# Moving two weight loads, one attention output and one LayerNorm by a visit in a fused transformer block

## Chip, cores and metric

One NeuronCore of a Trainium2 chip runs the whole program. The metric is the device time of one execution in microseconds (us). The kernel before took a median of 360.95 us in three runs (360.5 to 361.54).

## What is computed

A pre-norm block: dilated sliding-window attention, then an MLP, each with a residual. S = 2048 tokens, D = 576, 32 heads of 18, F = 4608, all arrays bf16.

```python
def _A_ref(x, wqkv, wo):            # H = 32, W = 8, dilation 2
    q, k, v = (x @ wqkv) ...        # per head
    idx = pos[:, None] - arange(W) * 2      # 8 keys for each token, 2 apart; below 0 masked
    attn = softmax(sum_d(q * k[idx]) * Dh ** -0.5)
    return sum_w(attn * v[idx]) @ wo

def _B_ref(x, w1, b1, w2, b2):
    h = gelu(layernorm(x) @ w1 + b1)
    return h @ w2 + b2

h  = x + _A_ref(layernorm(x), wqkv, wo)
h2 = h + _B_ref(layernorm(h), w1, b1, w2, b2)
```

## The kernel before, in words

**Tiles.** The 2048 tokens are 16 tiles of 128: tile j holds tokens 16p + j on partition p. With a dilation of 2 the eight keys of a token of tile j lie in the tiles of the same parity: at the same partition for tiles up to j, one partition lower for those above. So attention works on a ring of eight tiles (`kv_ring`, one for even and one for odd j), takes the tiles from 14 downwards, and when a tile is done its K and V are replaced by the same rows shifted by one partition, which `halo` (L344) loads from a copy in DRAM (`store_halo`). A halo row is issued by SP when DVE has read the old row, and the next tile's product waits for it.

**Stages.** The first stage makes Q, K and V of all tiles on PE in 24 *visits*, numbered 0 to 23, and meanwhile the attention of the first group (tiles 14 and 12, called A[0] and A[1]) and part of that of A[2]. Then eight groups of two tiles go through the MLP; while PE works on one group, DVE, ACT and the DMAs do the attention and the LayerNorm (LN2) of the next. LN1 of the even tiles is turned on PE (`tr_x`); the odd tiles, normalized on ACT, go to DRAM (`out_x`, L290) and come back transposed, two tiles at a time (`in_x`, L295). Visits 12 to 23 use the odd tiles; the last read, `in_x(3)`, serves visits 21 to 23.

**A visit** (`visit`, L242) works on two or three *pairs*. A pair is one 128x576 product in two PSUM banks; since the contraction is split over two halves of the array's rows, it is done in two halves (`phase`, L221): 10 matmuls, and 8 more in which the banks have changed places. All first halves come first, then a hook (transposes on PE), then the second halves, each followed by the evacuation of its pair on ACT, and by the functions of `between` (behind the first, or the n-th with `{n: ...}`). Because the banks change places, a second half has to stand behind the end of the first. This is done by a *marker* (L237): a no-op on POOL's queue that waits for the last matmul of the first half, and that the first matmul of the second half waits for:

```python
def marker(mm_ins):
    nop = nc.gpsimd.nop().ins
    tc.add_manual_dep(nop, mm_ins.name, sync_dep, reason="end of a half's visit")
```

**Order.** The whole kernel stands in a manual schedule: each engine runs its instructions in the order in which the Python code emits them. For the first stage the order is written in tables by visit: `after` (L944) holds what follows a visit, `loads` (L937) the weight loads issued behind that, `between` (L967), `hooks` (L976), and `wo_with` (L975), which adds the pair of an output projection to a visit. SP issues nearly all DMAs, in order. A weight load also waits for the last evacuation emitted before it (`pace`, L103).

**What the change touches.**
- `load_w1(c)` (L131), c = 0 to 5: 768 KB each. Before, pieces 3 and 4 follow visit 13, piece 5 visit 17.
- Attention output of A[1]: DVE writes o to `q_all` (L414); `o_tail` (L197) copies its last 128 columns on ACT; `tr_o` (L431) turns o on PE into PSUM pair D, and ACT copies it to `oT`. `wo_duo` (L449) multiplies by Wo, also into pair D (`pw`).
- LN2 of A[1]: `ln2` (L478) on DVE adds x to `pw` (`h`, L473) and makes the statistics (L148 to L155) and the negative mean (L487); `ln2_rstd` (L529) makes one power on POOL (L161); `ln2_norm` (L537) scales the mean (L539) and writes `hn` (L174) on ACT; `tr_h` (L554) turns it on PE, ACT copies it to `hnT` (L557), which the MLP of the first group needs.
- QK of A[2] on DVE: the product (`att_qk_a`, L352), four adds (`att_qk_add`, L361), logits, maximum, difference (`att_qk_rest`, L377), then the exponential on ACT (`att_exp`, L393).
- Warm-up matmuls on a constant (`busy`, L833) ahead of the first transposes.

Behind the first stage: `late_wo` and `wo_visit` in the first group's MLP are the output projections of the second group's tiles; their `oT` comes by a store and a transposed read (`dma_tr_o`, L216).

Of the kernel before, what the change touches and what calls it, by code (L numbers as in the profile page):

```python
# [17 lines left out]
def kernel(  # L18
# [12 lines left out]
    nc = tc.nc  # L31
    P = 128
    _, S, D = A_x.shape
# [62 lines left out]
    def psum_pair(tag, name, dtype=F32):  # L96
        n = 512 if dtype == F32 else 1024
        return psum.tile([P, 2, n], dtype, tag=f"ps{tag}", name=name)
# [78 lines left out]
    def transpose_in(pair, src, tail=None):  # L177
        for kt in range(KT):
            c = min(kt * P, D - P)
            block = src[:, c:c + P] if kt < KF or tail is None else tail  # L180
            for r in range(2):
                nc.tensor.matmul(pair[:, r, kt * HP:(kt + 1) * HP], lhsT=block[half_rows(r)],
                                 rhs=ident[half_rows(r), half_rows(r)], start=True, stop=True, skip_group_check=True)
# [17 lines left out]
    def turned(dst, pair, k0=0, k1=KT):  # L201
        return dict(out=dst[:, k0:k1, :].rearrange("p k (r t) -> p r k t", r=2),
                    in_=pair[:, :, k0 * HP:k1 * HP].rearrange("p r (k t) -> p r k t", t=HP))
# [14 lines left out]
    def half_rows(r):  # L218
        return slice(r * HP, (r + 1) * HP)
# [51 lines left out]
    def new_xnT(js):  # L271
        t = qp.tile([P, KT, 2 * P], BF16, tag="xnT", name="xnT", bufs=5)
        for n, j in enumerate(js):
            xnT[j] = t[:, :, n * P:(n + 1) * P]
        return t

    def tr_x(j, tag):
        pair = psum_pair(tag or "CAB"[(ring_pos[0] + 1) % 3], "xt_pt")
        transpose_in(pair, q_all[:, j, :])
        if EVEN.index(j) % 2 == 0:  # L280
            new_xnT(EVEN[EVEN.index(j):][:2])
        for k0, k1 in ((0, 2), (2, KT)) if j in EVEN[0:2] else ((0, KT),):
            nc.scalar.copy(**turned(xnT[j], pair, k0, k1))
# [24 lines left out]
    def qkv_duo(j, t):  # L308
        def make():
            ps = ring_pair("pq")  # L310
            xt = xnT[j]

            def op(g, i, sl, kt):
                c0 = g * HALF
                if g == 0 and kt == KF - 1 and sl.start:
                    kt = KF
                return xt[sl, kt, :], (wq_sb[sl, kt, t * D + c0:t * D + c0 + HALF] if kt < KF else wqh_sb[sl, t, c0:c0 + HALF])

            def evac():
                dst = (q_all[:, j, :], k_ring[j % 2][:, j // 2, :], v_ring[j % 2][:, j // 2, :])[t]  # L320
                scale = dict(scale=rstd_of[j]) if j in EVEN else {}
                pace[0] = nc.scalar.activation(out=dst.rearrange("p (d g h) -> p g d h", g=2, h=H // 2),
                                               in_=ps[:, :, 0:HALF].rearrange("p g (h d) -> p g d h", h=H // 2),
                                               func=ACT.Copy, **scale).ins
                if j == ATT_ORDER[0] and t == 1:
                    store_halo(j, slice(0, 1))
            return dict(g=[[ps[:, r, 0:HALF]] for r in range(2)], op=op, evac=evac)
        return make
# [12 lines left out]
    def logit_of(js):  # L341
        return logits[:, sides(js)]
# [15 lines left out]
    def att_qk_add(j, steps):  # L358
        for o, a, c in steps:
            n = (c - a if c < 9 else 9) * H  # L360
            nc.vector.tensor_tensor(out=prod[:, :, o * H:o * H + n], in0=prod[:, :, a * H:a * H + n],  # L361
                                    in1=prod[:, :, c * H:c * H + n], op=ALU.add)

    def att_qk_b(j, i, skip=0):
        side[j] = i
        out = logit_of([j])[:, 0]
        att_qk_add(j, ((0, 0, 9), (0, 0, 4), (0, 0, 2), (0, 0, 1))[skip:])
        nc.vector.tensor_tensor(out=out, in0=prod[:, :, 0:H], in1=prod[:, :, 8 * H:9 * H], op=ALU.add)
        if j // 2 + 1 < W:
            nc.vector.memset(out[0:1, j // 2 + 1:W, :], -1e9)  # L370
# [332 lines left out]
    def c_(fn, *a):  # L703
        return lambda: fn(*a)
# [96 lines left out]
    def call(fns):  # L801
        for fn in fns:
            fn()

    with tc.manual_schedule(engines={ENG.PE, ENG.Activation, ENG.DVE, ENG.SP, ENG.Pool}):
# [23 lines left out]
        load_w1h()  # L829
        busy = psum_pair("D", "busy")  # L830
        ones = nc.const_aps.tensor(1.0, [P, 512], BF16)
        for n in [512] * 8 + [P] * 5:
            nc.tensor.matmul(busy[:, 0, 0:n], lhsT=ones[:, 0:P], rhs=ones[:, 0:n], start=True, stop=True)  # L833
        nc.gpsimd.memset(mhalf[:], -0.5)
        nc.gpsimd.memset(eps2[:], EPS * EPS)
# [37 lines left out]
        def ln1_even_rstd(*gis):  # L873
            for gi in gis:
                mv, _ = ln1.pop(gi)
                veps = qp.tile([P, 1], F32, tag="ln1_veps", name="ln1_veps", bufs=8)
                nc.vector.tensor_scalar(out=veps[:], in0=mv[:, 0, 1:2], scalar1=1.0, scalar2=EPS, op0=ALU.mult, op1=ALU.add)
                rstd_of[EVEN[gi]] = ln_rstd(veps, f"ln1_{gi}", 1)[:, 0:1]
# [20 lines left out]
        A = ATT_ORDER  # L899
# [35 lines left out]
            ln2_ins(c, d)  # L935

        loads = {}  # L937
        for c, v in enumerate((2, 3, 4, 13, 13, 17)):
            loads[v] = loads.get(v, []) + [c_(load_w1, c)]
        for q, v in enumerate((6, 8, 11, 12)):  # L940
            loads[v] = [c_(load_wo, [q])]
        for n, v in enumerate((19, 19, 20, 20, 21, 22)):
# [11 lines left out]
                c_(store_halo, A[1]), c_(store_halo, A[0], slice(1, 2))],  # L954
            9: [c_(ln1_act, 9, 0)],
            10: [c_(att_pv, A[0]), c_(ln1_act, 9, 1), c_(in_x, 1), c_(halo, A[1], 1)],
            11: [c_(out_x, 2), c_(halo, A[0], 2)],
            12: [c_(ln1_act, 10, 0)],
            13: [c_(ln1_act, 10, 1), c_(in_x, 2), c_(out_x, 3), c_(store_halo, A[2]), c_(store_halo, A[3])],
            14: [c_(att_pv, A[1]), c_(in_x, 3), c_(load, b2_bc, B_b2.partition_broadcast(P))],  # L960
            15: [c_(halo, A[1], 2), c_(o_tail, A[0])],
            17: [c_(o_tail, A[1]), c_(ln2, A[0]), c_(att_qk_a, A[2])],
            18: [c_(ln2_rstd, A[0]), c_(halo, A[2], 1)],
            19: [c_(ln2, A[1])],
            20: [c_(ln2_rstd, A[1]), c_(att_qk_rest, A[2], 0)],
        }
        between = {  # L967
            10: [c_(att_exp, A[0])],
            13: [c_(att_exp, A[1])],
            18: {1: [c_(tr_o, A[1], "D")]},  # L970
            19: {1: [c_(ln2_norm, A[0])]},
            21: [c_(ln2_norm, A[1])],
            22: [c_(att_exp, A[2])],
        }
        wo_with = {17: A[0], 19: A[1]}  # L975
        hooks = {  # L976
            0: {1: lambda: call([c_(tr_x, EVEN[1], "C"), c_(ln1_even, 2)])},
            **{n: {m: c_(tr_x, EVEN[2 * n + m - 1], "D" if m == 1 else None) for m in (1, 2)} for n in (1, 2, 3)},
            12: c_(tr_b1, "D"),
            16: c_(tr_o, A[0], "D"),  # L980
            21: c_(tr_h, A[0], "D"),
            22: c_(tr_h, A[1], "D"),
        }
        seq = [(j, t) for t in (1, 2) for j in EVEN[:2]] + [(j, 1) for j in EVEN[2:]] \
            + [(j, 0) for j in A[0:2]] + [(j, 2) for j in EVEN[2:]] + [(j, 0) for n in (0, 4, 2) for j in EVEN[n:n + 2]] \
# [1 line left out]

        ln1_even_rstd(0, 1)
        tr_x(EVEN[0], "D")
        for qd in range(len(seq) // 2):  # L990
            duos = [qkv_duo(*seq[2 * qd]), qkv_duo(*seq[2 * qd + 1])]
            if qd in wo_with:
                duos.append(wo_duo(wo_with[qd], "D"))
            visit(duos, hooks.get(qd), between.get(qd, ()), apart=qd == 0)
            call(after.get(qd, ()))
            call(loads.get(qd, ()))
# [37 lines left out]
        for k, g in enumerate(GROUPS):  # L1034
            c, d = GROUPS[k + 1] if k + 1 < len(GROUPS) else (None, None)
# [123 lines left out]
```

## Time and profile before

| what | value |
|---|---|
| median of 3 runs | 360.95 us (360.5 to 361.54) |
| profiled execution | 362.23 us, of which the profile's span is 360.4 |
| mean granted PE clock | 0.995 |
| busy: PE, DVE, ACT, POOL | 352.6, 295.9, 235.9, 48.1 us |
| PE busy in 0 to 10 us | 7.55 us |
| PE busy in 52.5 to 68.2 us | 13.68 of 15.70 us |
| start of the first MLP matmul | 68.15 us |

All times in the views count from the start of the span. A timeline row has start, length, engine, source line, operation, output and input, count, and in brackets the time for which the engine was idle ahead of it and what ended that. SPq is the queue of DMAs issued by SP: the length of its rows is that of the issue, not of the transfer. The chain that ended last is followed back from the last instruction; each piece is work on the step that set the end. In the table of stages each row has a window, its length, and the busy time of each engine in it, the granted clock of PE, the share of the 16 DMA engines that was busy, and GB/s.

### The profile page before, as it was taken

Reading aid. Unit: us, or ns where it says so; the run is one execution under the profiler, and the core shown is the slowest. Engines: PE = TensorE matmul, PEld = TensorE weight load, DVE = VectorE, ACT = ScalarE, POOL = GpSimd, SP = SyncE. Lnnn points to the kernel's source line nnn. Section 1 sums busy time; section 2 is a strip of 40 time slices with the busy share of each in tenths; the row PEclk is TensorE's granted clock in tenths of the full one; section 3 lists DMA queues with packets and bytes.
Section 4 is the critical chain, followed back from the end, with each engine's and each line's share of the span. In section 5 each row is a group of like instructions: output and inputs, shape, how many; then the busy total and the mean of one; then the engine's idle time right before and its main releaser. Section 6 shows DMA issues by size and latency. Waiting matters only on the chain.

```text
span 360.4 us, 11550 instructions
## 1 busy us (share of the span) xinstructions
PE 352.6 (98%) x4938; PEld 290.7 (81%) x4938; DVE 295.9 (82%) x416; ACT 235.9 (65%) x524; POOL 48.1 (13%) x61
## 2 busy tenths in 40 slices
PE   7999998999999999999999999999999999999996
PEld 3788886788778877887788778877887788778874
DVE  5999999989889998998799899989998989520431
ACT  4889764898556783668656956695669566706620
POOL 2340005000212020201110202021102110210000
PEclk8999999999999999999999999999999999999999
DMA  7996599972636496732463355344545254283001
GB/s 240 329 294 193 147 258 310 367 253 55 169 66 100 132 244 109 129 79 51 91 102 90 85 124 84 90 86 120 88 90 99 58 85 58 54 120 51 4 1 34
DMA packets 63492, 46.29 MB, mean 128 GB/s; under 512 B 32192, under 2 KB 61760, under 8 KB 63440
## 3 DMA queue, kind: packets, MB, share of 16 engines
q1 hardware_dynamic: 59472, 41.50, 43.6%
q0 software_dynamic: 3744, 3.84, 9.9%
q8 instruction: 38, 0.62, 0.8%
q10 hardware_dynamic: 224, 0.22, 0.3%
q14 instruction: 14, 0.11, 0.1%
HBM read 23.38 MB, written 12.42 MB: 99 GB/s over the span
## 4 chain that ended last, share of the span: by engine, by line
PE 80%; DVE 11%; DMA 5%; ACT 2%; issue 1%; SPq 0%; DVEq 0%; ACTq 0%
PE pm L228 39%; PE po L691 25%; PE po L603 10%; PE pw L228 4%; DMA xnT<-xd 3%; DVE ln_stats L148 2%; DVE prod L361 2%; DVE prod L407 1%; DVE prod L352 1%; PE pq L228 1%; DMA x_all<-in_A_x_dram 1%; DMA wq_sb<-in_A_wqkv_dram 1%; ACT h_all L584 1%; DVE prod L413 1%; DVE ln_mv L149 1%
## 5 line engine op out<-in xcount | busy, mean ns | idle before, releaser
L228 PE MATMUL pm<-hnT,w_sb 64*128 64x256 bf16 x2304 | 143.0, 269 | 0.0
L584 ACT ACTIVATE h_all<-pm,b_sb 128x256 f16<-128x256 f32 (+1 forms) x288 | 108.7, 496 | 51.0 <-PE pm L228 50.3
L228 PEld LDWEIGHTS <-w_sb 64*128 64x128 bf16 x2304 | 111.6, 94 | 15.2 <-issue 1.7
L228 PE MATMUL pq<-wq_sb,xnT 64*128 64x288 bf16 x720 | 55.7, 286 | 3.0 <-DMA xnT<-xd 1.8
L691 PEld LDWEIGHTS <-h_all 128*128 128x128 f16 x480 | 46.2, 98 | 13.7 <-issue 1.6
L228 PEld LDWEIGHTS <-xnT 64*128 64x128 bf16 x864 | 44.7, 95 | 11.9 <-DMA xnT<-xd 2.1
L361 DVE TENSOR_TENSOR prod<-prod 128x2304 bf16<-128x2304 bf16 (+1 forms) x64 | 44.2, 691 | 2.1
L352 DVE TENSOR_TENSOR prod<-kv_ring,q_all 128x4608 bf16<-128x4608 bf16 x16 | 40.8, 2551 | 3.2 <-POOL ln_rstd L498 2.4
L407 DVE TENSOR_TENSOR prod<-kv_ring,probs 128x4608 bf16<-128x4608 bf16 x16 | 40.9, 2558 | 2.2 <-DMA kv_ring<-kv_dram 1.7
L228 PE MATMUL pm<-hnT,w1h_sb 64*128 64x256 bf16 x288 | 39.2, 269 | 0.0
L691 PE MATMUL po<-w2a_sb,h_all 128*128 128x288 bf16 (+1 forms) x262 | 35.9, 286 | 0.0
L413 DVE TENSOR_TENSOR prod<-prod 128x2304 bf16<-128x2304 bf16 (+1 forms) x32 | 33.9, 1058 | 1.1
L603 PEld LDWEIGHTS <-h_all 128*128 128x128 bf16 x288 | 27.9, 98 | 7.9 <-issue 0.9
L691 PEld LDWEIGHTS <-kv_ring 128*128 128x128 f16 x252 | 24.6, 98 | 6.3
L603 PE MATMUL po<-w2a_sb,h_all 128*128 128x288 bf16 x224 | 28.5, 286 | 0.0
L228 PE MATMUL pq<-wqh_sb,xnT 64*128 64x288 bf16 x144 | 28.1, 288 | 0.0
L793 POOL DMA_DIRECT2D x_all<-o_sb x12 | 10.7, 888 | 125.1 <-PE pw L228 72.3
L498 POOL TENSOR_TENSOR ln_rstd<-ln_var,mhalf 128x1 f32<-128x1 f32 x13 | 10.2, 786 | 84.2 <-ACT ln_var L497 84.2
L161 POOL TENSOR_TENSOR ln_rstd<-ln_veps,mhalf 128x1 f32<-128x1 f32 (+2 forms) x14 | 14.1, 1019 | 45.4 <-DVE ln_nmean L487 28.0
L691 PE MATMUL po<-w2b_sb,h_all 128*128 128x288 bf16 (+1 forms) x122 | 19.7, 286 | 0.2 <-DVE h_all L671 0.2
L228 PE MATMUL pw<-wo_sb,oT 64*128 64x288 bf16 x256 | 19.5, 283 | 0.0
L671 DVE TENSOR_TENSOR kv_ring<-h_all 128x1536 f16<-128x1536 f16 (+3 forms) x9 | 6.8, 760 | 15.4 <-ACT h_all L584 15.3
(113 smaller groups left out, 400.3 us busy)
## 6 DMA issues: line engine op xcount, KB each, us to landing
w_sb<-in_B_w_dram SPq DMA_DIRECT2D x6, 768.0 KB, 6.3
kv_ring<-kv_dram SPq DMA_DIRECT2D x28, 144.0 KB, 2.4
kv_dram<-kv_ring SPq DMA_DIRECT2D x13, 288.0 KB, 4.3
x_all<-in_B_b_dram SPq DMA_DIRECT2D x15, 144.0 KB, 3.8
w2a_sb<-in_B_w_dram SPq DMA_DIRECT2D x2, 1008.0 KB, 7.1
td<-q_all SPq DMA_DIRECT2D x14, 144.0 KB, 2.3
td<-hn SPq DMA_DIRECT2D x14, 144.0 KB, 1.8
x_all<-h POOLq DMA_DIRECT2D x14, 144.0 KB, 4.5
```

The source lines that it names most:

```text
L148: nc.vector.bn_stats(out=stats[:, i, c, :], in_=src[:, c * HALF:(c + 1) * HALF])
L161: nc.gpsimd.tensor_tensor(out=rstd[:], in0=veps[:], in1=mhalf[:].to_broadcast([P, n]), op=ALU.pow)
L228: last = nc.tensor.matmul(duo["g"][r ^ swap][i], lhsT=lhsT, rhs=rhs, start=(swap == 0 and i == 0 and kt == 0), stop=(swap == 1 and kt == K ...
L352: ins = nc.vector.tensor_tensor(out=prod[:], in0=k_ring[j % 2], in1=q_all[:, j, :].unsqueeze(1) .to_broadcast([P, W, D]), op=ALU.mult).ins
L361: nc.vector.tensor_tensor(out=prod[:, :, o * H:o * H + n], in0=prod[:, :, a * H:a * H + n], in1=prod[:, :, c * H:c * H + n], op=ALU.add)
L407: nc.vector.tensor_tensor(out=prod[:].rearrange("p w (d h) -> p w d h", h=H), in0=v_ring[j % 2].rearrange("p w (d h) -> p w d h", h=H), in ...
L413: nc.vector.tensor_tensor(out=prod[:, 0:n, :], in0=prod[:, 0:n, :], in1=prod[:, n:2 * n, :], op=ALU.add)
L498: ins = nc.gpsimd.tensor_tensor(out=rstd[:], in0=var[:], in1=mhalf[:], op=ALU.pow).ins
L584: pace[0] = nc.scalar.activation(out=hT(grp)[:, f, 0:N], in_=ps[:, r, i * N:(i + 1) * N], func=ACT.Gelu_apprx_tanh, bias=b1_sb[:, f:f + 1] ...
L603: nc.tensor.matmul(banks[half], lhsT=hT(grp)[:, f, i * P:(i + 1) * P], rhs=w2_rows(f)[:, half * HALF:(half + 1) * HALF], start=(f == 0), s ...
L691: nc.tensor.matmul(bank, lhsT=l, rhs=r, start=start, stop=stop, skip_group_check=True)
L793: nc.gpsimd.dma_start(out=x_of(j), in_=o_of.pop(j), accum_op=ALU.add)
```

## The change

1. W1 piece 3 is issued behind visit 11, right behind `out_x(2)`; piece 4 behind visit 14, after `in_x(3)`. Piece 5 stays at 17.
2. `o_tail` of A[1] moves from the end of visit 17 into visit 18, behind the first pair's evacuation; `tr_o` of A[1] from the end of visit 18 into the hook of visit 19; its wo pair from visit 19 to visit 20.
3. `ln2` of A[1] moves from behind visit 19 to behind visit 20, ahead of its rstd. The first of the four adds of QK of A[2] moves ahead of it (behind visit 18).
4. `tr_h` of A[0] and A[1] move from the hooks of visits 21 and 22 to those of 22 and 23; `ln2_norm` of A[1] from visit 21 to visit 22, behind the exponential of A[2].
5. The warm-up has three more matmuls of 128 columns, and twelve of 64 rows and 128 columns follow the first transposes (`tr_x`).

```diff
+    ADDS = ((0, 0, 9), (0, 0, 4), (0, 0, 2), (0, 0, 1))
 def att_qk_b(j, i, skip=0):
-        att_qk_add(j, ((0, 0, 9), (0, 0, 4), (0, 0, 2), (0, 0, 1))[skip:])
+        att_qk_add(j, ADDS[skip:])
...
-        for n in [512] * 8 + [P] * 5:
+        for n in [512] * 8 + [P] * 8:
             nc.tensor.matmul(busy[:, 0, 0:n], lhsT=ones[:, 0:P], rhs=ones[:, 0:n], start=True, stop=True)
...
-        for c, v in enumerate((2, 3, 4, 13, 13, 17)):
-            loads[v] = loads.get(v, []) + [c_(load_w1, c)]
+        for c, v in ((0, 2), (1, 3), (2, 4), (4, 14), (5, 17)):
+            loads[v] = [c_(load_w1, c)]
...
-            11: [c_(out_x, 2), c_(halo, A[0], 2)],
+            11: [c_(out_x, 2), c_(load_w1, 3), c_(halo, A[0], 2)],
...
-            17: [c_(o_tail, A[1]), c_(ln2, A[0]), c_(att_qk_a, A[2])],
-            18: [c_(ln2_rstd, A[0]), c_(halo, A[2], 1)],
-            19: [c_(ln2, A[1])],
-            20: [c_(ln2_rstd, A[1]), c_(att_qk_rest, A[2], 0)],
+            17: [c_(ln2, A[0]), c_(att_qk_a, A[2])],
+            18: [c_(ln2_rstd, A[0]), c_(halo, A[2], 1), c_(att_qk_add, A[2], ADDS[:1])],
+            20: [c_(ln2, A[1]), c_(ln2_rstd, A[1]), c_(att_qk_rest, A[2], 0, 1)],
         between = {
...
-            18: {1: [c_(tr_o, A[1], "D")]},
+            18: [c_(o_tail, A[1])],
             19: {1: [c_(ln2_norm, A[0])]},
-            21: [c_(ln2_norm, A[1])],
-            22: [c_(att_exp, A[2])],
+            22: [c_(att_exp, A[2]), c_(ln2_norm, A[1])],
-        wo_with = {17: A[0], 19: A[1]}
+        wo_with = {17: A[0], 20: A[1]}
         hooks = {
...
             16: c_(tr_o, A[0], "D"),
-            21: c_(tr_h, A[0], "D"),
-            22: c_(tr_h, A[1], "D"),
+            19: c_(tr_o, A[1], "D"),
+            22: c_(tr_h, A[0], "D"),
+            23: c_(tr_h, A[1], "D"),
...
         tr_x(EVEN[0], "D")
+        busy = psum_pair("B", "busy")
+        for n in range(12):
+            sl = half_rows(n % 2)
+            nc.tensor.matmul(busy[:, n % 2, 0:P], lhsT=ones[sl, 0:P], rhs=ones[sl, 0:P], start=True, stop=True)
```

## Prediction

> **What bounds the kernel now.** I read the page first. PE is busy for 352.6 of 360.4 us, so 7.8 us of idle PE is all that a change of order can win. The stages table puts 2.5 of these in the first 10 us, 2.0 between 52.5 and 68.2, and 3.1 at the end, which the change does not touch. Next I read the chain that ended last, in order of time:
>
> ```profile
> 50.88 0.13 DVE prod L413
> 51.01 9.39 DMA xnT<-xd
> 60.44 1.40 PE pq L228 x20
> ```
>
> Until 50.88 the chain is DVE work almost alone (from 10.52, where x landed). Then one transfer, the last transposed read of the odd x tiles, takes 9.39 us, and PE starts visit 21 on it. From 68.32 to 339.68 the chain is PE without a gap. SP's timeline tells why the transfer is slow (start, length, what):
>
> ```profile
> 48.84 2.00 SPq L104 DMA_DIRECT2D w_sb<-in_B_w_dram  x2
> 51.01 3.86 SPq L296 DMA_TRANSPOSE xnT<-xd  x1
> ```
>
> Two W1 pieces (768 KB each) go out just ahead of it. The other three reads of this kind landed 3.6 to 3.8 us after issue. In PE's timeline (last bracket: idle time ahead of the row and who ended it) I mark the slips between 52 and 68 us:
>
> ```profile
> 52.85 0.29 PE L182 MATMUL o_pt<-ident,q_all 64*128 64x64 bf16 x8
> ...
> 60.44 0.66 PE L228 MATMUL pq<-wq_sb,xnT 64*128 64x288 bf16 x8 [1.75 <-DMA xnT<-xd]
> ...
> 64.56 0.29 PE L188 MATMUL h_pt<-ident,hn 64*128 64x64 bf16 x8
> ...
> 68.15 0.60 PE L228 MATMUL pm<-hnT,w_sb 64*128 64x256 bf16 x8
> ```
>
> A full half of a visit's pair (10 matmuls) takes 0.615, a second half (8) 0.49, tr_o 0.14, tr_h 0.39. Adding these from 52.53, the three starts are late by 0.32 (the copy of o's tail on ACT ends at 52.46), 1.93 (the transfer) and 0.28 (LN2's output from ACT, 64.51): 2.53 us of slip. The first MLP matmul stands at 68.15.
>
> **W1 pieces.** The fourth goes behind out_x(2), at about 39.8, where SP would have stood idle until 42.79; the stages of 40 to 42 and 42 to 44 us show a DMA share of 0.63 and 0.09, room for about 2.5 us of transfer, and 768 KB at the 385 GB/s of the full stages is 2.0 us. The fifth goes behind the read. The read is then issued when out_x(3) has landed (47.25 + 2.5 = 49.75) and lands near 53.5 to 55; PE asks at 58.2. So the 1.93 goes. The sixth leaves SP at about 52.6 in place of 56.0. The stream of W2 that follows kept the DMA full until 77 us; with 2 us of it moved ahead and its first parts earlier, it is drained near 74. That matters at two later rows of DVE:
>
> ```profile
> 63.60 2.56 DVE L352 TENSOR_TENSOR prod<-kv_ring,q_all 128x4608 bf16<-128x4608 bf16 x1 [0.47 <-DMA kv_ring<-kv_dram]
> ...
> 79.77 2.56 DVE L407 TENSOR_TENSOR prod<-kv_ring,probs 128x4608 bf16<-128x4608 bf16 x1 [0.97 <-DMA kv_ring<-kv_dram]
> ```
>
> Halo rows that took 6.9 and 4.9 us; in quiet stages the same transfer takes 2.1 to 2.6. I take both waits as gone.
>
> **o of the second tile a visit later.** tr_o moves from the end of visit 18 into visit 19, behind both first halves (53.76). o's tail is then copied behind the first evacuation of visit 18, done at 53.1: the 0.32 is gone. Visit 19 starts at 52.53, has no wo pair, and ends at 54.89; visit 20 has three pairs, ends at 58.20, and its pw starts its last half at 57.71. DVE's h began 0.70 after such a start at 93.1, so h of the second tile begins at 58.41 (56.53 before).
>
> **DVE.** The first add (1.37 us by the chain's row at 27.27) is moved ahead of h: DVE has it done at 57.97 and then idles 0.44. h to veps took 56.53 to 58.56; it now ends at 60.44. The three adds left, logits, maximum and difference follow, and the maximum is subtracted at 63.61 in place of 63.10.
>
> **The new wait.** Each second half of a pair waits for a marker, a no-op on POOL's queue behind the last matmul of the first half. POOL's queue is in order: at 12.41 an ln_rstd whose input was ready at 12.11 starts only when the PE work of the marker ahead of it is done. The order of instructions has the rstd of the second tile behind the markers of visit 20 and ahead of those of visit 21, as before; but before, visit 21 stood on the DMA until 60.44 and the rstd had started at 58.65:
>
> ```profile
> 54.17 2.86 POOL L161 TENSOR_TENSOR ln_rstd<-ln_veps,mhalf 128x1 f32<-128x1 f32 x1 [26.38 <-DVE ln_nmean L487]
> 58.65 1.66 POOL L161 TENSOR_TENSOR ln_rstd<-ln_veps,mhalf 128x1 f32<-128x1 f32 x1 [1.62 <-DVE ln_nmean L487]
> ```
>
> Now POOL stands on veps until 60.5, while PE has both first halves of visit 21 done at 59.43. What is queued behind are visit 21's two markers, and PE's second halves wait for them. The run of the rstd itself does not hold them: the 2.86 at 54.17 did not stop PE's second half at 54.83. So PE goes on at 60.65: **1.2 us new**.
>
> From there: visit 22 at 61.63, tr_h of the first tile at 62.87, second halves 63.25, visit 23 at 64.23, both first halves done 65.46. tr_h of the second tile needs hn from ACT, whose order is now: evacuation of visit 22's first pair (to 64.50), exp (0.31 to the next), nmean (0.32), hn (0.87), done at 66.0. So tr_h at 66.05, **0.6 us new**. Its copy on ACT (behind one evacuation, 66.5 to 67.2) hides behind the two second halves, and the MLP starts at 66.05 + 1.39 = 67.44. **Sum: 2.53 removed, 1.2 + 0.6 added: 0.7 us earlier.**
>
> **Can the rest keep it?** The next place where PE waits for others is the wo pair of the next group's second tile, and it had no slack:
>
> ```profile
> 91.80 0.48 PEld L228 LDWEIGHTS <-oT 64*128 64x128 bf16 x10 [0.24 <-DMA oT<-td]
> ```
>
> This oT is the end of DVE's chain (o done 84.92, store, transposed read landed 91.64). DVE's chain starts at 63.65 in place of 63.60 and loses the 0.97 at 79.77: 0.9 us earlier, just enough for PE's 0.7. The first tile's oT landed at 83.2 for a use at 84.86: slack 1.4. Behind that, h of the second tile waits for pw (0.87 at 93.82), so DVE moves with PE, and the later stages are unchanged.
>
> **Fillers.** Three more 128-column matmuls and twelve of 64 rows lie in the gaps at 4.30 to 4.83 and 5.15 to 5.87. The granted clock is 1.00 until 6.9, 0.50 from there to 10.3 (3.4 us), then 1.00: PE work worth 1.7 us is lost. If the fillers prevent that, PE comes to visit 16 earlier and waits there: its tr_o (45.90) needs o of the first tile, which DVE ends at 45.51 and whose tail ACT ends at 45.84, and DVE is busy for 40.1 of the 42 us from 10 on and waits for PE nowhere. At most 0.1 gets through. If the fillers are slow (0.107 each as the cold ones at 3.6), the first matmuls start 0.56 late and meet the second weight piece (6.66) 0.2 late, and as PE has no idle time from 10 to 52, that costs 0.2. I take 0.
>
> **Rivals.**
> 1. The marker is not held (or briefly). Then PE waits only for hn: exp follows DVE at 63.7, hn ends at 65.2, the MLP starts at 66.65, 1.5 earlier; oT above gives 0.9, or up to 1.5 if its store lands in the 2.4 us of its neighbour at 77.86 rather than 3.3. 359.5 to 360.0. Against it: the 12.41 row.
> 2. The clock is the bound. [...] As a mechanism of this kernel: all of the 1.7 us comes through on top of the 0.7, 358.6. Against it: DVE's chain at 45.5.
> 3. The halo of V at 74.8 is still late (DMA full until 77). oT then comes 0.05 later than before, PE waits for it, and nothing is left: 361.0.
> 4. The read is no earlier, because the fourth piece only moves the queue: same 361.0. Against it: the free DMA at 42 to 44.
> 5. Slower: the fourth W1 piece holds up the halo of V for the second tile (issued 42.79, landed 45.3, used by DVE at 46.89). W1 pieces landed 5.2 to 8.0 us after issue, so this one by 45.0 to 47.8, and the halo behind it by up to 48.8. DVE has 0.44 to spare at 58: a landing after 47.3 eats the gain, after 48.0 the kernel is slower, by 0.1 to 0.8: 361.1 to 361.8. [...]
>
> **Numbers.** The profiled execution took 362.23 (span 360.4 and 1.8 around it), 1.3 above the median of the runs, 360.95. 0.7 less gives 361.5 for it, 360.2 for the median. Chances: forecast 0.47, rival 1 0.20, rival 2 0.07, rivals 3 and 4 together 0.18, rival 5 0.08. A measurement of this kernel can tell about 0.3%, 1.1 us, from no change. Faster by more: most of rivals 1 and 2 that goes past 1.1, and a tail of the forecast, 0.26. Slower by more: the end of rival 5 and mishaps that I have not named, 0.07. Range: the forecast with 0.4 either way for the medians, stretched to rival 1's end below and to rivals 3 and 4 and the lower half of 5 above: 359.1 to 361.4.
>
> **What would show it.** Right: the read lands within 6 us of issue; PE's slips at 52.85 and 60.44 are gone and a wait on POOL's queue of 1 to 1.4 us stands in visit 21; tr_h in visit 23 waits for hn by about 0.6; MLP at 67.4; no halo wait at 79.8; oT of the second tile near 90.8. Wrong: visit 21 runs through; a wait on kv_ring near 46.9; PE waiting over 0.3 us near 91; a PE that reaches 45.9 early and does not wait.

## The result and the profile after

The change makes the kernel slower: a median of 362.75 us in 22 runs (361.91 to 363.49), against 361.74 us for the kernel before in 22 runs (360.22 to 363.21). The ratio is 1.0029, with a 95% interval of 1.0017 to 1.0041: 1.0 us lost where 0.7 was forecast as won.

The profiled execution of the changed kernel does not show this loss. Its span is 359.9 us, 0.5 less than the 360.4 of before, and nearly every step in it came out as forecast. In PE's timeline, the rows that answer to those of before, with the last matmuls ahead of the wait:

```profile
53.27 0.28 PE L182 MATMUL o_pt<-ident,q_all 64*128 64x64 bf16 x8
...
53.78 0.66 PE L228 MATMUL pq<-wq_sb,xnT 64*128 64x288 bf16 x7 [0.20 <-POOLq L238]
...
58.69 0.65 PE L228 MATMUL pq<-wq_sb,xnT 64*128 64x288 bf16 x8
59.18 0.28 PE L228 MATMUL pq<-wqh_sb,xnT 64*128 64x288 bf16 x2
60.45 0.66 PE L228 MATMUL pq<-wq_sb,xnT 64*128 64x288 bf16 x7 [0.98 <-POOLq L238]
...
65.84 0.29 PE L188 MATMUL h_pt<-ident,hn 64*128 64x64 bf16 x8 [0.42 <-ACT hn L174]
...
67.23 0.60 PE L228 MATMUL pm<-hnT,w_sb 64*128 64x256 bf16 x8
```

Visit 21 no longer waits for the transfer; it stops in its middle. By the pace of a full half (0.615), the second half was due at 59.30 and starts at 60.45, 1.15 late, and what ends the wait is POOL's queue at the marker's line, L238. `tr_h` of the second tile was due at 65.26 and comes 0.58 late. POOL's own timeline has the instruction that the marker stands behind, and DVE's the input that this instruction waits for:

```profile
53.75 2.86 POOL L161 TENSOR_TENSOR ln_rstd<-ln_veps,mhalf 128x1 f32<-128x1 f32 x1 [26.43 <-DVE ln_nmean L489]
60.41 1.00 POOL L161 TENSOR_TENSOR ln_rstd<-ln_veps,mhalf 128x1 f32<-128x1 f32 x1 [3.80 <-DVE ln_veps L155]
```

```profile
58.28 0.76 DVE L475 TENSOR_TENSOR h<-pw,x_all 128x576 f32<-128x576 f32 x1 [0.70 <-PE pw L228]
...
60.17 0.15 DVE L155 TENSOR_SCALAR ln_veps<-ln_mv 128x1 f32<-128x1 f32 x1
...
63.42 2.55 DVE L352 TENSOR_TENSOR prod<-kv_ring,q_all 128x4608 bf16<-128x4608 bf16 x1
...
79.12 2.56 DVE L409 TENSOR_TENSOR prod<-kv_ring,probs 128x4608 bf16<-128x4608 bf16 x1 [0.51 <-DMA kv_ring<-kv_dram]
```

The power starts 0.09 after the end of `ln_veps`, and PE 0.04 after that: the marker has passed as soon as the power has *begun*.

The first rows of PE and POOL show the same wait a second time, in visit 19, where the forecast has none. The second halves there were due at 53.41, when `tr_o` (0.14) is done, and start at 53.78, 0.03 after the power of the *first* tile's LN2. The wo pair has left this visit, so its first halves end before that power can start. The MLP start is near the forecast's 67.44 all the same, because PE came to visit 19 at 52.04 and not at 52.53. That agreement is in part luck.

SP's queue shows both moved W1 pieces, and a read that lands 3.4 us after its issue at 50.54:

```profile
38.91 0.53 SPq L104 DMA_DIRECT2D w_sb<-in_B_w_dram  x1
42.32 0.34 SPq L347 DMA_DIRECT2D kv_ring<-kv_dram  x1
...
50.54 1.33 SPq L296 DMA_TRANSPOSE xnT<-xd  x1
51.97 0.52 SPq L104 DMA_DIRECT2D x_all<-in_B_b_dram  x1
52.54 0.43 SPq L104 DMA_DIRECT2D w_sb<-in_B_w_dram  x1
```

So one execution of each kernel says "0.5 us less", and the medians say "1.0 us more". The spans of all 22 runs tell why: those of the changed kernel go from 359.9 to 361.7 with a median of 360.9, and the profiled one is the lowest of them. (Its device time is nevertheless 362.68, since 2.8 us lie around its span; around 20 of the 22 it is 1.7 to 2.0.) The profile of before, at 360.4, is an execution above the middle: in the runs of the kernel before that stand beside the experiments, in four groups, spans range from 358.3 to 364.0, with medians of 359.3 to 360.1.

### The profile page after: what moved, and what is told of

Same layout as the page of the kernel before. It is cut to its first block, busy times and chain, and to the rows that moved or that the text cites. A ratio compares the mean times of both kernels' runs of the same rounds, so it can differ in the third digit from the quotient of the medians.

```text
span 359.9 us, 11578 instructions
## 1 busy us (share of the span) xinstructions
PE 353.6 (98%) x4953; PEld 289.1 (80%) x4953; DVE 295.9 (82%) x416; ACT 236.0 (66%) x524; POOL 47.4 (13%) x61
## 4 chain that ended last, share of the span: by engine, by line
PE 94%; issue 2%; ACT 2%; DMA 1%; DVE 1%; POOLq 0%; ACTq 0%
PE pm L228 38%; PE po L693 25%; PE pq L228 13%; PE po L605 10%; PE pw L228 5%; PE busy L835 1%; ACT h_all L586 1%; DMA oT<-td 1%; PE xt_pt L182 0%; DVE kv_ring L673 0%; ACT hn L174 0%; ACT q_all L322 0%; DVE h_all L673 0%; PE o_pt L182 0%; PE busy L994 0%
## 5 line engine op out<-in xcount | busy, mean ns | idle before, releaser
L228 PE MATMUL pq<-wq_sb,xnT 64*128 64x288 bf16 x720 | 54.6, 283 | 1.3 <-POOLq L238 1.2
L228 PEld LDWEIGHTS <-xnT 64*128 64x128 bf16 x864 | 42.4, 94 | 11.7 <-POOLq L238 2.0
L500 POOL TENSOR_TENSOR ln_rstd<-ln_var,mhalf 128x1 f32<-128x1 f32 x13 | 10.2, 785 | 82.0 <-ACT ln_var L499 82.0
```

Of the source, the lines that this page charges most:

```text
L228: last = nc.tensor.matmul(duo["g"][r ^ swap][i], lhsT=lhsT, rhs=rhs, start=(swap == 0 and i == 0 and kt == 0), stop=(swap == 1 and kt == K ...
L500: ins = nc.gpsimd.tensor_tensor(out=rstd[:], in0=var[:], in1=mhalf[:], op=ALU.pow).ins
```

## The experiments

Three theories stood against each other at one point or another. **V**: the 1.9 us wait of before, for the last odd x read, is there only in some executions, so that removing it wins less than one profile shows. **M**: the marker behind the power costs about 1 us in *every* execution of the changed kernel. **H**: the fourth W1 piece, now ahead of V's halo and of Wo on SP, delays these. The kernel before ran beside each, with medians of 361.08 (the parts of the change), 361.60 (the piece behind the halo), 361.64 (the power later, the two that build on it, and the fifth piece alone) and 361.91 (the fourth piece back, the changed kernel again, and the fillers added to the fifth piece). Because it spreads so widely, most ratios to it have intervals of about 0.2% either way; spans and traces tell more.

### The parts of the change, one by one

**Without the fillers** (the changed kernel with both groups of warm-up matmuls taken out):

```diff
-        for n in [512] * 8 + [P] * 8:
+        for n in [512] * 8 + [P] * 5:
...
-        busy = psum_pair("B", "busy")
-        for n in range(12):
...
```

> The changed kernel with the warm-up of before (13 matmuls, no fillers behind the first transposes); the reordering of visits 11 to 23 and the W1 moves stay. Theory F (the fillers and the longer warm-up cost the time that the change lost, the reordering gains what its profile shows): 0.5 to 0.9 us faster than before, the MLP starts 0.5 to 0.9 earlier. Theory R (the reordering or what follows it costs it, the fillers are absorbed): as the changed kernel, 1.0 us slower than before.

Measured: 362.89 (361.99 to 363.8), ratio to before 1.0049, interval 1.003 to 1.0067; about the changed kernel's own time. Its trace is the first to show theory H. Timelines of DVE and of PE:

```profile
48.37 2.56 DVE L409 TENSOR_TENSOR prod<-kv_ring,probs 128x4608 bf16<-128x4608 bf16 x1 [1.46 <-DMA kv_ring<-kv_dram]
```

```profile
49.47 0.65 PE L228 MATMUL pw<-wo_sb,oT 64*128 64x288 bf16 x7 [0.50 <-DMA wo_sb<-in_A_wo_dram]
...
62.34 0.66 PE L228 MATMUL pq<-wq_sb,xnT 64*128 64x288 bf16 x7 [0.97 <-POOLq L238]
```

The fourth W1 piece was issued at 40.17 here. DVE waits 1.46 us for V's halo rows, which stand behind it, PE waits for Wo, which stands behind both, and the marker costs its 0.97 just the same, later.

**The fillers alone** (the kernel before with both groups of warm-up matmuls):

> The kernel before with the longer warm-up and the twelve fillers only. Theory F: about 1.0 us or more slower than before, and its first PE transposes start later than 4.8 us. Theory R: within 0.3 us of before, since PE waits at the first tr_o (45.9) for DVE whatever it won at the start.

Measured: 361.98 (359.74 to 363.73), ratio 1.001, interval 0.9985 to 1.0034. No difference that can be measured; its spread is as wide as that of before, and its trace has the read landing after 9.0 us and 1.37 us of wait in visit 21.

**The W1 pieces alone** (the kernel before with the loads of the change):

```diff
-        for c, v in enumerate((2, 3, 4, 13, 13, 17)):
+        for c, v in ((0, 2), (1, 3), (2, 4), (4, 14), (5, 17)):
...
-            11: [c_(out_x, 2), c_(halo, A[0], 2)],
+            11: [c_(out_x, 2), c_(load_w1, 3), c_(halo, A[0], 2)],
```

> The kernel before with only the two W1 pieces moved. The read of the last odd tiles lands early, visit 21 starts at 58.5 and its second halves wait for nothing (the rstd of the second tile is ready by then), so the slip of 1.93 us goes and 0.6 stays: MLP start 1.5 to 1.9 earlier. Then the output projection of the second tile at 91 waits for oT and gives back what is over 0.9. Theory F and R1 (the moved LN2 is what costs): 0.9 us faster than before. Theory R2 (the W1 pieces cost, through DMA contention): 0.3 to 1.0 slower than before.

Measured: 361.36 (360.43 to 362.75), ratio 1.0001, interval 0.9975 to 1.0027: nothing won, though the wait for the read is gone. DVE's timeline, then PE's:

```profile
48.34 2.56 DVE L407 TENSOR_TENSOR prod<-kv_ring,probs 128x4608 bf16<-128x4608 bf16 x1 [1.47 <-DMA kv_ring<-kv_dram]
```

```profile
54.30 0.29 PE L182 MATMUL o_pt<-ident,q_all 64*128 64x64 bf16 x8 [0.71 <-DVE h L473]
...
67.67 0.60 PE L228 MATMUL pm<-hnT,w_sb 64*128 64x256 bf16 x8
```

The halo rows took 5.5 us, o of the second tile is late by that, and `tr_o` stands on it: one wait exchanged for another.

**The moves of o and LN2 alone** (the kernel before with parts 2 to 4 of the change, the loads and the warm-up as before):

> The kernel before with only the attention output and LN2 of the second tile a visit later (no W1 moves, no fillers). The read of the last odd tiles still lands near 60.4, and now tr_h of both tiles stands a visit later: MLP start at 60.45 + 2.2 (visit 21) and the rest as before, 0.3 to 0.6 us earlier than before by the o copy and the missing wait for hn, and oT at 91 gives that back: all theories within 0.4 us of before, except R1 (the moved LN2 costs): 0.5 to 1.0 slower.

Measured: 361.94 (361.23 to 362.97), ratio 1.0017, interval 0.9998 to 1.0035; the spread of spans shrinks to 359.5 to 361.2. The read took 7.1 us, and nobody waited for it; the marker's wait is 0.98, that for LN2's output 0.42, and the MLP starts at 67.73. So the moves alone bring M in full.

### How steady is the wait that the change removes?

More executions of the two kernels as they are, profiled one by one.

> The kernel before, one more profiled execution. Theory V (the wait for the last odd read that the first profile shows, 1.75 us at visit 21, is one outcome among several: the read lands 7 to 9.4 us after issue and is wanted 7.5 after it, so many executions have no stall there): a span near 358.5 has visit 21 running on at once, a span of 360 or more has the wait. Theory C (the wait is in every execution): the 1.4 to 1.9 us idle ahead of visit 21 is there whatever the span.

> The kernel before, a further profiled execution, as the one before it: theory V says that idle time ahead of visit 21 and the span go together; theory C that the wait is always there.

> The changed kernel, one more profiled execution. Theory M (the marker wait in visit 21 is in every execution, whatever else varies): 0.9 to 1.3 us idle at the second halves of visit 21 and about 0.5 ahead of the last tr_h, again. Theory H (the fourth W1 piece ahead of the V halo is what costs): the DVE product at 46.5 to 48.5 waits up to 1.5 us for the halo, as in the run without fillers, and the MLP starts at 68 or later.

Measured: 360.43 (span 358.7) and 362.34 (span 360.5) for the kernel before, 361.67 (span 359.9) for the changed one. PE's timeline in the first of these executions of before:

```profile
58.49 0.28 PE L228 MATMUL pq<-wqh_sb,xnT 64*128 64x288 bf16 x1
58.64 0.66 PE L228 MATMUL pq<-wq_sb,xnT 64*128 64x288 bf16 x8
...
66.35 0.60 PE L228 MATMUL pm<-hnT,w_sb 64*128 64x256 bf16 x8
```

and in the second:

```profile
60.52 0.66 PE L228 MATMUL pq<-wq_sb,xnT 64*128 64x288 bf16 x8 [1.49 <-DMA xnT<-xd]
...
68.23 0.60 PE L228 MATMUL pm<-hnT,w_sb 64*128 64x256 bf16 x8
```

The same kernel, the same read behind the same two W1 pieces: issued at 51.29 and landed after 7.3 us in the first, issued at 51.94 and landed after 8.5 in the second. PE asks at about 58.6, so the first runs through and the second stands. That is theory V. The changed kernel repeats 0.98 for the marker and 0.42 for LN2's output, to the digit.

### The fourth piece behind the halo

The changed kernel, with the piece one place later on SP:

```diff
-            11: [c_(out_x, 2), c_(load_w1, 3), c_(halo, A[0], 2)],
+            11: [c_(out_x, 2), c_(halo, A[0], 2), c_(load_w1, 3)],
```

> The changed kernel with the fourth W1 piece behind the V halo of visit 11 instead of ahead of it, so that the halo has nothing large ahead; the two Wo loads and the odd read stay behind the piece. Theory H: the halo lands 2.5 us after issue, DVE waits for nothing at 46.9, 0.5 to 1.3 us faster than the changed kernel, that is within 0.4 us of before. Theory M: the marker wait stays, within 0.3 us of the changed kernel, 0.8 to 1.3 slower than before. If the piece now holds up Wo (first used at 48.3), PE waits there and nothing is won either.

Measured: 364.16 (363.46 to 366.26), ratio 1.0079, interval 1.0049 to 1.0109: worse. The halo is in time now, since it is issued at 42.58 and the piece behind it, at 42.97; but Wo, which follows, is not. PE's timeline:

```profile
49.47 0.65 PE L228 MATMUL pw<-wo_sb,oT 64*128 64x288 bf16 x7 [1.25 <-DMA wo_sb<-in_A_wo_dram]
51.21 0.28 PE L228 MATMUL pw<-woh_sb,oT 64*128 64x288 bf16 x1 [1.08 <-DMA woh_sb<-in_A_wo_dram]
```

In these traces the small transfers issued behind the large load come late: V's halo by 1.46 us and Wo by 0.50 without the fillers, V's halo by 1.47 with the W1 pieces alone, Wo by 1.25 and 1.08 here.

The waits for Wo are only part of this loss. Behind them, after a stretch (48.0 to 51.3) in which PE was busy for 0.97 of 3.3 us, eight matmuls take PE 0.96 us at 52.68 and again at 53.64, where 0.49 is its pace: about half the clock from about 51.7 to 55.1, an estimate from PE's rows. Three of the seven runs, this one among them, have a mean granted clock of 0.995 and spans of 363.6 to 364.2; the other four have 1.00 and spans of 361.7 to 362.4.

### Taking the suspected waits away one after the other

**M alone.** The changed kernel with one instruction moved: the power is emitted behind the first evacuation of visit 21, so that it stands behind that visit's markers on POOL.

```diff
-            20: [c_(ln2, A[1]), c_(ln2_rstd, A[1]), c_(att_qk_rest, A[2], 0, 1)],
+            20: [c_(ln2, A[1]), c_(att_qk_rest, A[2], 0, 1)],
...
+            21: [c_(ln2_rstd, A[1])],
             22: [c_(att_exp, A[2]), c_(ln2_norm, A[1])],
```

> The changed kernel, with one instruction moved: the power on POOL that makes LN2's rstd of the second tile (L161) is emitted behind the first evacuation of visit 21 and no longer ahead of visit 21's markers. Theory M (a wait of 1.0 to 1.3 us in visit 21 for a marker that stands in POOL's queue behind this power, in every execution): no wait on POOL's queue in visit 21, the MLP starts 0.6 to 1.0 us earlier than in the changed kernel (67.2 to 67.4 there), about 66.4, and the median is 0.5 to 1.0 us below the changed kernel's 362.75, that is about even with the kernel before. Theory H (the loss is the fourth W1 piece ahead of the halo rows of V and of Wo): the wait in visit 21 goes, but the median stays within 0.4 us of the changed kernel, since DVE is late anyway and the wait for LN2's output in visit 23 grows by as much.

Measured: 361.69 (361.19 to 363.4), ratio 1.0001, interval 0.9979 to 1.0022; the median span is 359.9, 1.0 below the changed kernel's. The two ran in different groups; each against the kernel before beside it, the difference is 0.8, and the intervals of their two ratios still overlap a little. Visit 21 runs through. The profiled execution has the longest span of the twelve (361.6) and shows H once more, with M gone. DVE, then PE:

```profile
48.41 2.56 DVE L409 TENSOR_TENSOR prod<-kv_ring,probs 128x4608 bf16<-128x4608 bf16 x1 [1.64 <-DMA kv_ring<-kv_dram]
```

```profile
49.10 0.65 PE L228 MATMUL pw<-wo_sb,oT 64*128 64x288 bf16 x7 [0.77 <-DMA wo_sb<-in_A_wo_dram]
51.79 0.66 PE L228 MATMUL pq<-wq_sb,xnT 64*128 64x288 bf16 x8 [0.46 <-DMA xnT<-xd]
...
67.04 0.29 PE L188 MATMUL h_pt<-ident,hn 64*128 64x64 bf16 x8 [0.82 <-ACT hn L174]
```

**M and H.** As that, with the fourth piece behind visit 13 again:

```diff
-        for c, v in ((0, 2), (1, 3), (2, 4), (4, 14), (5, 17)):
+        for c, v in ((0, 2), (1, 3), (2, 4), (3, 13), (4, 14), (5, 17)):
...
-            11: [c_(out_x, 2), c_(load_w1, 3), c_(halo, A[0], 2)],
+            11: [c_(out_x, 2), c_(halo, A[0], 2)],
```

> As the kernel in which the power is moved behind visit 21's first evacuation, and the fourth W1 piece (index 3) is loaded behind visit 13 again, as before; the fifth stays behind the last odd x read. Theory H (the fourth piece holds up V's halo and Wo, in part of the executions, by up to 1.5 and 0.5 us): 0.4 to 1.0 us below the kernel with the power moved alone, and below the kernel before by 0.5 us or more. If only theory M holds: within 0.3 us of the kernel with the power moved alone.

Measured: 361.25 (360.52 to 362.55), ratio 0.9984, interval 0.9961 to 1.0008; median span 359.45, another 0.45 less. No wait for halo or Wo; the MLP starts at 66.66, with 0.82 of wait for LN2's output left.

**That wait too.** As the last, with `between[22]` turned round: `ln2_norm` of the second tile ahead of the exponential of the third.

> As the one with the fourth piece back and the power moved, and on ACT the LN2 output of the second tile is made ahead of the exponential of the third tile. PE's wait for LN2's output in visit 23 (0.42 to 0.72 us in the changed kernel) goes, and the MLP starts 0.3 to 0.7 us earlier, near 66.0. The exponential comes 1.2 us later, but DVE first makes a product of 2.56 us and its adds before it needs it, so DVE loses nothing. The median is 0 to 0.5 us below the kernel without this edit; all of it only if oT of the second tile, near 91 us, comes no later than PE does.

Measured: 361.10 (360.36 to 362.48), ratio 0.9981, interval 0.9959 to 1.0003. The MLP starts at 65.74, 0.9 earlier, and the median gains 0.15, which the spread does not tell from nothing. Where the rest goes is in PE's timeline:

```profile
83.15 0.66 PE L228 MATMUL pw<-wo_sb,oT 64*128 64x288 bf16 x8 [0.42 <-DMA oT<-td]
91.63 0.66 PE L228 MATMUL pw<-wo_sb,oT 64*128 64x288 bf16 x8 [0.25 <-POOLq L238]
```

PE comes early to both wo pairs of the next group and waits, at the first for `oT`, at the second for a marker that stands behind the power of the next LN2 on POOL (L500, started at 91.57). The chain that leads there is DVE work from the product at 64.44 to `h` at 88.72, then LN2 on ACT. So in this trace the MLP starts earlier than DVE can follow. The product at 64.44 itself waited 1.00 us for a halo row, so that a part of this wait may be absent in other executions.

**H with M left in.** The changed kernel with only the fourth piece behind visit 13 again, and the changed kernel itself beside it:

> The changed kernel with the fourth W1 piece (index 3) loaded behind visit 13 again, the fifth behind the last odd x read; the power on POOL stays ahead of visit 21's markers. If the loss is the sum of a marker's wait (theory M, 1.0 us) and of the fourth piece ahead of V's halo and Wo (theory H, about 0.4 us): the marker's wait of 1.0 to 1.3 us stands in visit 21, no wait for V's halo or Wo, and the median lies 0.3 to 0.6 us below the changed kernel and still 0.3 to 0.8 us above the kernel before. If the fourth piece costs nothing: within 0.2 us of the changed kernel.

> The changed kernel again, as a measure beside the two others: 1.0 us above the kernel before, spans of 359.9 to 361.7.

Measured: 362.21 (361.65 to 363.77), ratio 1.0004, interval 0.998 to 1.0028, against 362.82 (361.83 to 363.33), ratio 1.0017, interval 0.9992 to 1.0042. Median spans 360.3 and 360.9: the early piece costs 0.6 here, 0.45 in the pair above. The intervals overlap, so that H's *size* rests on two differences of the same sign, and its mechanism on the rows. The kernel with M left in also gives M a second time: its median span is 0.85 above that of the kernel with the power later and the fourth piece back (0.65, each against the kernel before beside it). The trace of the changed kernel beside it has H's rows; DVE, then PE:

```profile
47.18 2.56 DVE L409 TENSOR_TENSOR prod<-kv_ring,probs 128x4608 bf16<-128x4608 bf16 x1 [0.56 <-DMA kv_ring<-kv_dram]
```

```profile
50.55 0.67 PE L228 MATMUL pq<-wq_sb,xnT 64*128 64x288 bf16 x8 [0.40 <-DMA xnT<-xd]
...
61.15 0.66 PE L228 MATMUL pq<-wq_sb,xnT 64*128 64x288 bf16 x7 [0.98 <-POOLq L238]
...
67.94 0.60 PE L228 MATMUL pm<-hnT,w_sb 64*128 64x256 bf16 x8
```

The piece was issued at 38.85, within 0.1 of the first profile of this kernel, where the halo was in time. Over the six traces with the piece ahead of the halo, the halo is late by 0, 0.56 and 0 us where the piece is issued at 38.61, 38.85 and 38.91, and by 1.64, 1.46 and 1.47 where it is issued at 39.65, 40.17 and 40.43. The forecast had it at about 39.8. The read with 0.40 is the *third* odd x read, which takes 5.6 us behind the piece, halo and Wo.

### The one edit that wins

The kernel before, with only the fifth piece behind the last read:

```diff
-        for c, v in enumerate((2, 3, 4, 13, 13, 17)):
+        for c, v in enumerate((2, 3, 4, 13, 14, 17)):
```

> The kernel before, with only one W1 piece (index 4) moved from behind visit 13 to behind visit 14, where it is issued behind the last odd x read. Theory V (the kernel before loses 1.4 to 1.9 us at that read in some executions only, because two pieces of 768 KB are ahead of it): the read lands within 7 us of issue in every execution, visit 21 starts without a wait, the MLP starts at 66.3 to 66.7, spans lie near 358.5 in all executions where those of the kernel before spread from 358.4 to 362, and the median falls by 0.5 to 1.0 us below the kernel before. Rival (the spread of the kernel before has another cause, the read is not it): the spread of spans stays as wide as that of the kernel before and the medians agree within 0.3 us.

Measured: 360.72 (359.94 to 361.29), ratio 0.9957, interval 0.9934 to 0.998, the best of all kernels. The 12 spans lie between 358.2 and 359.5, median 358.9; the 35 of the kernel before beside it between 358.3 and 363.5, median 359.9. The best executions are no better than before; the bad ones are gone. Visit 21 runs through, and the MLP starts at 66.47. This is theory V a second time: the spread of before goes when that one load is moved. The wait in the traces (at most 1.75) is not all of it. Of the 111 runs of the kernel before in the four groups, seven have spans of 362.0 or more, and all seven have a mean granted clock of 0.994 or less; there is no trace of any of them, so how the read and the clock hang together there is not shown. (The trace's longest read took 7.0 us, and again nobody waited.)

With the fillers added to it:

> The kernel before with only the W1 piece of index 4 moved behind the last odd x read, and the fillers of the change. If the early clock dip costs nothing, because DVE's chain sets when tr_o of the first tile can start: within 0.3 us of the kernel with the piece moved alone, that is 0.7 to 1.0 us below the kernel before. Rival (the dip is worth up to 1.7 us of PE): 1 us or more below that.

Measured: 361.49 (360.19 to 362.61), ratio 0.9982, interval 0.9957 to 1.0007. That is 0.42 below the kernel before beside it, where 0.7 to 1.0 was expected. The trace has the earliest MLP start of all, 65.70, but its span, 359.2, is one that others reach from a later start. The fillers bring nothing that the times show; whether they cost something is open, as the two intervals overlap.

### All traces in one table

The waits are those in PE's brackets, in us, the marker's in visit 21. A bracket is some 0.17 below the slip that PE's pace gives (0.98 and 1.15), and it leaves out small slips. The last column is the median of all spans of that kernel.

| kernel | wait for last read | for marker | for LN2's output | MLP starts | span of this trace | median span |
|---|---|---|---|---|---|---|
| before, profile | 1.75 | 0 | 0 | 68.15 | 360.4 | 359.3 to 360.1 |
| before, second profile | 0 | 0 | 0 | 66.35 | 358.7 | |
| before, third profile | 1.49 | 0 | 0 | 68.23 | 360.5 | |
| fillers only | 1.37 | 0 | 0 | 67.67 | 360.1 | 359.55 |
| fifth piece moved only | 0 | 0 | 0 | 66.47 | 359.5 | 358.9 |
| fifth piece moved, fillers | 0 | 0 | 0 | 65.70 | 359.2 | 359.5 |
| W1 pieces only | 0 | 0 | 0 | 67.67 | 360.4 | 359.55 |
| o and LN2 moves only | 0 | 0.98 | 0.42 | 67.73 | 360.0 | 360.15 |
| changed, profile | 0 | 0.98 | 0.42 | 67.23 | 359.9 | 360.9 |
| changed, second profile | 0 | 0.98 | 0.42 | 67.42 | 359.9 | |
| changed, last profile | 0 | 0.98 | 0.42 | 67.94 | 360.3 | 360.9 |
| changed, without the fillers | 0 | 0.97 | 0.42 | 69.13 | 361.5 | 361.1 |
| fourth piece behind the halo | 0 | 0.97 | 0.42 | 71.48 | 364.2 | 362.4 |
| fourth piece back | 0 | 0.97 | 0.42 | 67.64 | 360.3 | 360.3 |
| power later | 0 | 0 | 0.82 | 68.43 | 361.6 | 359.9 |
| power later, fourth back | 0 | 0 | 0.82 | 66.66 | 359.1 | 359.45 |
| and LN2's output first | 0 | 0 | 0 | 65.74 | 359.4 | 359.1 |

The span follows the start of the MLP to within about half a microsecond, until that is about 66.5. From the changed kernel down to the last row the median span falls by 1.0 (M; 0.8 against the kernel before beside each), 0.45 (H) and 0.35, to 359.1, which is about that of the kernel with the fifth piece moved alone. So the o and LN2 moves, freed of the two waits that were forecast, win nothing over that one edit.

## Why the prediction was wrong

**The step that failed is the last one: "0.7 less gives 361.5 for it, 360.2 for the median."** The 0.7 is 2.53 of slip removed less 1.8 of new waits, and 1.93 of the 2.53 is the wait for the read. I read that in one execution and took it away from the median as if every execution had it. It is 1.75, 0 and 1.49 us in the brackets of three traces of the kernel before. By the medians of the kernel with the fifth piece moved alone, its removal is worth 0.92 us (361.64 to 360.72), not 1.93; the ratio, 0.9957, would give 1.55, and its interval 0.7 to 2.4. The two new waits, on the other hand, are made by the order of instructions and by DVE's time, and are there in all seven traces that have the moves as they stand, whatever the DMAs do. With 0.9 in place of 1.93, 1.5 is removed and 1.8 added: 0.3 lost.

**Two more terms stood at nothing.** One is the wait in visit 19: "Visit 19 starts at 52.53, has no wo pair, and ends at 54.89" leaves no room for it. By PE's pace it is 0.33 to 0.37 in the three traces of the changed kernel, and PE starts 0.03 to 0.04 after the first tile's power in nine of the ten traces with the moves (a slip of 0.20 to 0.66). The prediction's own row has that power at 54.17, later than the 53.90 at which those second halves would have started. The other term is the fourth piece, at 0.45 to 0.6. The three add up to 1.05 to 1.2, against 1.0 measured; with so wide an interval on the read that is a fit and not a proof, and the exact shares stay open.

The first of these could have been asked from the one profile: the text notes that the profiled execution stands 1.3 above the median, and a wait on a DMA behind two large loads was a likely reason. The median of three, 360.95, was itself low: the larger groups of runs gave 361.1 to 361.9.

Point by point:

- *The marker's wait, 1.2 forecast:* 1.15 by PE's pace in the first trace of the changed kernel, and 0.97 to 0.98 in the brackets of all seven traces that have the power ahead of the markers. The reading that the marker is held until the power has started, and not until it is done, is right: PE goes on 0.04 after the start of a power that takes 1.00 (60.41, 60.45); rival 1 falls. Moving the power alone gave back 0.8 to 1.0 us of median span.
- *`tr_h` of the second tile, 0.6:* 0.58.
- *MLP start 67.44:* 67.23 in the first trace of the changed kernel, 67.42 and 67.94 in the two others. The unforeseen wait in visit 19 and PE's earlier arrival there nearly cancel in the first.
- *W1 pieces, the read by 53.5 to 55:* 53.9 in the first trace, so the fifth piece did its part. The *fourth* was the mistake in this item: "SP would have stood idle" was true of SP, and "room for about 2.5 us of transfer" was counted for the piece and not for what is issued behind it.
- *Rival 5, given 0.08:* its mechanism is there, in four of the six traces with the early piece ahead of the halo: V's halo late by 0.56, 1.46, 1.47 and 1.64 us, and in two of these Wo late as well, by 0.50 and 0.77. The rival also left out that Wo and the third odd x read stand in the same line. That the halo lands by up to 48.8, behind the piece, was an estimate; DVE went on at 47.18 to 48.41 in these four, and how much of the piece the halo waits for is not shown. Measured it costs 0.45 to 0.6 us of median. As a rival by itself it was to turn the forecast's gain into a loss of 0.1 to 0.8; in fact it came on top of a loss.
- *Both late halo rows gone:* the one at 63.6 is, in the three traces of the changed kernel; that at 79 waits 0.51, 0 and 0.43 instead of 0.97. The second profile of before has neither wait, so these too were not there in every execution.
- *oT near 90.8, "just enough":* PE's weight load for that pair is at 90.88. In the kernel with the fifth piece moved alone, whose MLP starts at 66.47, PE does wait for `oT` there (0.16, and 0.37 at the first tile's pair): the limit is real.
- *Fillers 0:* no gain of the median in three comparisons. But "at most 0.1 gets through" is not what the traces show: `tr_o` of the first tile starts at 45.05 to 45.68 in the ten traces with fillers and at 45.76 to 46.39 in the seven without. PE waits there for o, as forecast, in four of the ten (0.22 to 0.24).
- *The chances:* the 0.67 left for "no change" and the 0.07 for "slower" came from cases that all used the one profiled execution as their base. None of the rivals was "the wait that goes was not always there". It needed no new fact of the chip, only the question.

**Not settled:** what decides whether V's halo is late when the fourth piece is issued before 39 (it was in time in two traces and 0.56 late in a third), and why the last read lands after 7.3 us in one execution of before and 9.4 in another. Nor is the size of the wait in visit 19 in the median settled, since no run takes it away alone. The 0.35 us for LN2's output ahead of the exponential is by spans; by medians of time it is 0.15.

## What to carry to other kernels

Before a wait is counted as a gain, ask whether it is there in every execution: here the wait on a DMA that lands close to its deadline, behind large loads, was 1.75, 0 and 1.49 us in three executions of one program, while the wait that the order of instructions makes was 0.97 to 0.98 in all seven traces that have it, and the two may not be set against each other one to one. Take a second and third profile of the kernel before, or compare the profiled execution with the median and ask which wait the difference is. When a large load is moved into a gap of a queue, list the transfers issued behind it and their deadlines, since here they, and not the issuing engine, paid for it (V's halo up to 1.64 us late, Wo up to 1.25); and an instruction on a queue that also carries another engine's markers belongs behind the markers, unless its input is ready (moving the power there took the 0.98 out of visit 21). When work is taken out of a stretch, ask which wait its length had hidden (0.33 to 0.37 in visit 19 here).

## What was unexpected of the hardware

- The clock dip of the profiled execution (granted clock 0.50 from 6.9 to 10.3 us) was the exception. Of seven traces of kernels without fillers it is in that one alone. Such a dip would lower the mean granted clock by 0.005 (an estimate: 1.7 of 360 us); of the 111 runs of the kernel before beside the experiments 20 have 0.995 or less. Of the 107 runs of kernels with the fillers, leaving aside the one with the piece behind the halo, none is below 0.998: no mean among them shows such a dip, and the median gains nothing by it. The tables of stages of the first and the third profile of before (window, its length, busy time of PE, PEld, DVE, ACT and POOL, clock, DMA share, GB/s):

```profile
3.40:6.90 3.50, 1.87 (x26) 1.11 (x25) 2.67 (x10) 1.59 (x5) 0.54 (x1) 1.00 0.97 312
6.90:10.30 3.40, 3.29 (x38) 1.82 (x35) 2.70 (x8) 1.50 (x3) 0.55 (x2) 0.50 1.08 351
```

```profile
3.40:6.90 3.50, 2.26 (x26) 1.27 (x25) 2.67 (x10) 1.58 (x5) 0.47 (x1) 1.00 1.01 321
6.90:10.30 3.40, 3.29 (x57) 1.96 (x55) 2.61 (x8) 1.89 (x4) 0.62 (x2) 1.00 1.08 346
```

  With PE busy for 1.87 of 3.5 us the clock was halved in the next stretch, with 2.26 it was not. That the execution without the dip has the longer span of the two (360.5 against 360.4) fits the forecast that the dip is hidden behind DVE's chain.
- The last odd x read, behind two 768 KB loads, landed 7.3, 8.5 and 9.4 us after its issue in three executions of one program, issued at 51.29, 51.94 and 51.01. Waits made by order alone, the marker's in visit 21 and that for LN2's output, repeat to 0.01 us.
